# Pauses, loads and groups rearranged in the first quarter of a kernel for a 2-D transform and its experts

## The chip, the cores and the metric

The kernel runs on one core of a Trainium2 chip. What counts is the time of one execution on the device, in microseconds (us), smaller being better: the median of several runs. A kernel is compared with the kernel before on the same chip.

## The reference, cut to what matters

```python
def _attn_ref(x):                      # x: 8 batches, 2496 tokens, 256 columns
    X = np.fft.fft(x, axis=1)
    X = np.fft.fft(X, axis=2)
    return X.real.astype(np.float32)

def _moe_ref(x, w_gate, w1, w2):       # the 19968 tokens of the above, 8 experts, 1024 hidden
    logits = x @ w_gate
    expert_idx = np.argmax(logits, axis=1)
    ...                                # gate_w: the softmax value of the chosen expert
    for e in range(E):
        mask = expert_idx == e
        h = np.maximum(x[mask] @ w1[e], 0.0)
        out[mask] = gate_w[mask, None] * (h @ w2[e])
```

Every token is transformed, goes to the one expert with its largest logit, and its row comes back scaled.

## The kernel before, in words

**Transform.** A batch is folded by symmetry on VectorE (`fold_w`, `fold_fg`, `fold_z`, `fold_h`; lines 520 to 548), then multiplied along the sequence (S products, line 399, into two PSUM banks evicted by ScalarE's `ec` and VectorE's `pc`, `qc`, lines 452 to 464) and along the columns (D products, lines 758 to 767). A batch has two units, even and odd frequencies, so there are 16 units, numbered 0 to 15, each of 10 slots of 128 token rows. `load_x` (line 265) brings a batch in two DMAs of 1280 KB; there are two buffers for batches.

**Routing.** `route_a` and `route_b` find the expert of each token and its place in a list per expert; `place` (line 665) scatters each slot of 128 rows into `bucket` in HBM by an indirect DMA of GpSimd, ten of them a unit.

**Groups of tokens.** After units 2, 4, 7, 9, 11, 13, 15 and 16 a table says which rows of `bucket` make the next groups (`SEGS`: unit, width, number of groups). `first_row` and `group_rows` compute a table on VectorE, and `table_row` sends it to SyncE (line 1105), which reads registers from it (line 1124). The first four groups (0 to 3, `plain`) hold 128 rows, the next ten (4 to 13, "narrow" here) 256, later ones 512 ("tall"; from group 14 to 42 they are transposed on VectorE, line 1179, and not on TensorE). A group's rows are loaded by line 1136, its weights by line 1167 in eight parts of 256 KB, w1 and w2 of four parts each, into one buffer a part. So part p of the next group can be loaded only when this group has used its part p. The loads stand in SyncE's queue in program order, `x`, tables, rows and weights alike.

**Expert.** TensorE transposes the rows (line 1183), multiplies by w1 (line 1234 in plain groups; 1252 to 1254, three products of split operands, in others) and, two steps later, by w2 (1286; 1292 to 1295; 1302 and 1303). VectorE makes the low halves: `wal` of w1, `wb` of w2, `hl` of the hidden values, `xl` of the rows. `put` (line 1321) scatters the scaled rows to the output by indirect DMAs of GpSimd.

**Order.** In `start()`, units 0 to 3 and the first groups, the order on TensorE, VectorE and ScalarE is the program's own: `expert()` stands for one half step of the experts. After it `fft_until` steps are dealt between expert steps at a rate worked out from their counts, and a scheduler orders each engine's queue. Each engine takes its queue in order.

**Pauses of GpSimd.** `rest()` (lines 325 to 333) puts a fill of one element ahead of certain scatters and of each group's first `put`, and that fill waits until GpSimd's transfer before it has landed. `breath()` (lines 317 to 321) puts a fill of 128x1024 there, which waits for nothing, in units 1 to 3. Ahead of all, `start()` issues two indirect DMAs of no use to the result (`scrap`, line 809).

Of the kernel before, what the change touches and what calls it, by code (L numbers as in the profile page):

```python
# [22 lines left out]
P = 128  # L23
# [19 lines left out]
SEGS = [(2, 0.5, 4), (4, 1, 10), (7, 2, 4), (9, 2, 4), (11, 2, 5), (13, 2, 5), (15, 2, 5), (16, 2, 6)]  # L43
# [19 lines left out]
BLOCKED = 14, 43  # L63
PLAIN = 4
CUT = 2


def cuts():

    segs, used, g = [], 0, 0  # L70
    for n, w, count in SEGS:
        step, last = int(w * C), n == 2 * B
        rows = (n * H if g else int((~bad_slots()[:, : NE + CUT]).sum())) - used
# [151 lines left out]
def fft2_then_moe(ctx: ExitStack, tc: tile.TileContext, i: dict, out: bass.AP):  # L225
# [8 lines left out]
    scrap = dr.tile([S, P], I32, name="scrap")  # L234
# [73 lines left out]
    lull = cst.tile([1, 1], F32, name="lull")  # L308
    air = mo.tile([P, 2, 512], F32R, name="xl").bitcast(F32)
# [6 lines left out]
    def breath():  # L316

        last = ch["moved"]
        with tc.issue_after(last):
            pause = nc.gpsimd.memset(air, 0.0)  # L320
        return tc.issue_after(pause.ins)

    def rest():

        last = ch.get("moved")
        if not any(q is last for q in nc.cur_bb.bb.instructions):
            return nullcontext()
        with tc.issue_after(last):
# [4 lines left out]
        return tc.issue_after(pause.ins)  # L333
# [291 lines left out]
    def route_b(b, par, rb, st, fine=False):  # L625
# [14 lines left out]
        if (b, par) == (0, 1):  # L640
            ch["early"] = sc[:, :, CUT]
# [21 lines left out]
        def place(n, behind=None):  # L663
# [11 lines left out]
            tc.add_to_no_dep_group("sc1b" if u == 1 and n >= CUT else f"sc{u}", ins.ins)  # L675
# [19 lines left out]
    def groups_from(slots):  # L695

        return (["sc1b"] if slots <= NE + CUT else []) + [f"sc{q}" for q in range(-(-slots // NE), 2 * B)]

# [19 lines left out]
    def fft_steps():  # L718
# [88 lines left out]
        def start():  # L807
            for _ in range(2):
                nc.gpsimd.indirect_dma_start(
                    out=scrap[:, :],  # L810
                    out_offset=IndirectOffsetOnAxis(ap=ids[:, 0, 0:1].bitcast(U32), axis=0),
                    in_=ids.rearrange("p b n -> p (b n)")[:, 0:P],
                    in_offset=None,
                    bounds_check=S - 1,
                    oob_is_err=False,
                )
# [68 lines left out]
            pc = along_s_mm(2, 0)  # L885
            _, w, g0, count = cuts()[0]
# [5 lines left out]
            qc = along_s_mm(2, 1)  # L892
            pc()
# [6 lines left out]
            pc = along_s_mm(3, 0)  # L900
            st, rb = {}, cols.pop(2)
# [5 lines left out]
            qc = along_s_mm(3, 1)  # L907
# [18 lines left out]
            expert()  # L926
# [18 lines left out]
        for u, (b, par) in enumerate(units):  # L945
            if u < 4:
                continue
            if par == 0 and 2 <= b < B - 1:
                load_x(b + 1)
# [17 lines left out]
            yield from along_d(u)  # L967
# [47 lines left out]
    def group_rows(w, g0, count):  # L1015

        vec = nc.vector
        carry = ch["carry"]
# [110 lines left out]
    def load_rows(g):  # L1129
# [3 lines left out]
        xr = mo.tile([P, 4, RW], F32, name="xr", bufs=2)  # L1133
# [200 lines left out]
    def moe_steps(g0, g1):  # L1334
# [11 lines left out]
        if g0 == 0:  # L1346
            yield g0
# [4 lines left out]
        for n in range(len(units) + LAG):  # L1352
            if n < len(units):
                g, p, fs = units[n]
                more, half = g + 1 < g1, tall[g] == 1
                if p == 0 and fs[0] == 0 and more:
                    load_rows(g + 1)
# [44 lines left out]

    def begin():

        for g in first:
            rows_of[g] = ch["row", 2], NE + CUT
        next(moe)
# [7 lines left out]
    for n in sorted({s[0] for s in segs}):  # L1415
        todo = fft_until(n)
        if have:
            nf = FSTEPS * (n - rows_of[have[-1]][1] // NE)
# [33 lines left out]
        for g in have:  # L1452
            rows_of[g] = row, n * NE
# [29 lines left out]
```

## Time and profile before

| | |
|---|---|
| median of 3 runs | 1113.47 us (1109.48 to 1115.42) |
| the profiled execution | 1121.16 us |
| its span, first to last instruction | 1119.4 us |
| TensorE (PE) busy | 1066.6 us, 95% of the span |
| VectorE (DVE) busy | 810.1 us, 72% |
| ScalarE (ACT) busy | 592.2 us, 53% |
| GpSimd (POOL) busy | 359.4 us, 32% |
| mean granted clock of TensorE | 0.985 |

Busy time is a share of the whole span. The stages differ, so the sections below look at stretches of it. A row of the timeline gives start, duration, engine, source line, operation and tiles, and in square brackets how long the engine sat idle before it and what ended that. Duration of a merged row is from its first start to its last end.

### The profile page before, as it was taken

The numbers are of one execution on the slowest core, as the hardware profiler recorded it, in microseconds if no ns is written. First come the engines' busy times: TensorE is split into PE (matmuls) and PEld (weight loads), VectorE is DVE, ScalarE is ACT, GpSimd is POOL, SyncE is SP. The second block draws the span as 40 slices with busy tenths as digits, with TensorE's granted clock in tenths as the row PEclk, the third lists the DMA queues.
The fourth block names the chain that finished last, engine by engine and source line by source line (L and its number), as shares of the span: only waits on it lengthen the run. The fifth ranks groups of instructions, "written<-read, shape, count | busy, mean of one in ns | idle before, by whom it ended". The sixth has DMA issues, their size and how long they took to land.

```text
span 1119.4 us, 21641 instructions
## 1 busy us (share of the span) xinstructions
PE 1066.6 (95%) x6228; PEld 916.7 (82%) x6229; DVE 810.1 (72%) x1852; ACT 592.2 (53%) x1371; POOL 359.4 (32%) x407
## 2 busy tenths in 40 slices
PE   8686999999989999999999999999999999999997
PEld 4465898999878887888778887888888888899996
DVE  7745777977788698669766777678766666667775
ACT  2232465666554554455455555555555555466674
POOL 2754144541154235313531135311412111211111
PEclk9988999999999999999999999999999999999999
DMA  8559659745746466556564455445656555425511
GB/s 313 179 182 299 216 176 340 234 148 132 243 123 151 129 196 175 150 170 174 159 160 118 122 146 163 100 123 141 168 142 168 138 138 140 154 96 179 179 44 33
DMA packets 213431, 183.03 MB, mean 164 GB/s; under 512 B 150198, under 2 KB 153751, under 8 KB 211383
## 3 DMA queue, kind: packets, MB, share of 16 engines
q1 hardware_dynamic: 197171, 135.72, 45.0%
q0 software_dynamic: 15840, 45.67, 10.8%
q8 instruction: 51, 0.84, 0.3%
q14 instruction: 77, 0.63, 0.2%
q10 hardware_dynamic: 292, 0.17, 0.1%
HBM read 166.41 MB, written 45.07 MB: 189 GB/s over the span
## 4 chain that ended last, share of the span: by engine, by line
PE 82%; DVE 7%; DMA 4%; issue 3%; ACT 1%; SPq 1%; another core or an unknown queue 1%; POOL 0%; POOLq 0%; DVEq 0%; ACTq 0%
PE psY L1302 21%; PE psH L1253 12%; PE psH L1252 12%; PE psH L1254 11%; PE psY L1303 11%; PE psH L399 2%; PE psH L444 2%; PE psH L766 1%; PE psH L767 1%; DMA w1r<-w 1%; PE psY L1295 1%; PE psY L1294 1%; PE psY L1292 1%; DMA xr<-bucket 1%
## 5 line engine op out<-in xcount | busy, mean ns | idle before, releaser
L1302 PE MATMUL psY<-wb,hh 128*128 128x512 f32 x1088 | 397.6, 398 | 5.6 <-ACT hh L1257 2.3
L1321 POOL DMA_INDIRECT out<-ys,gt x160 | 165.2, 1033 | 446.1 <-DVE ys L1319 353.4
L1303 PE MATMUL psY<-wb,hl 128*128 128x256 f32 x1088 | 305.8, 281 | 0.2 <-DVE hl L1258 0.2
L1252 PE MATMUL psH<-xh,wah 128*128 128x512 f32 (+1 forms) x752 | 268.9, 358 | 3.1 <-ACT ec L452 1.7
L1253 PE MATMUL psH<-xl,wah 128*128 128x512 f32 (+1 forms) x752 | 264.6, 352 | 1.3 <-DVE xl L1193 1.1
L1254 PE MATMUL psH<-xh,wal 128*128 128x512 f32 (+1 forms) x752 | 262.5, 349 | 0.5 <-issue 0.3
L1302 PEld LDWEIGHTS psY<-wb,hh 128*128 128x128 f32 x1088 | 204.5, 188 | 52.4 <-issue 3.9
L1258 DVE SCALAR_TENSOR_TENSOR hl<-psH,hh 128x512 fp32r<-128x512 f32 (+1 forms) x320 | 215.1, 672 | 40.3 <-ACT hh L1257 34.5
L1257 ACT ACTIVATE hh<-psH 128x512 fp32r<-128x512 f32 (+1 forms) x320 | 187.7, 586 | 62.0 <-PE psH L1254 38.9
L665 POOL DMA_INDIRECT bucket<-rb,di x160 | 172.4, 1078 | 144.4 <-issue 65.3
L1303 PEld LDWEIGHTS psY<-wb,hl 128*128 128x128 f32 x1088 | 205.9, 189 | 8.4 <-DVE hl L1258 0.5
L1207 DVE TENSOR_TENSOR wal<-w1r,wah 128x512 fp32r<-128x512 f32 x188 | 129.5, 689 | 113.6 <-ACT wah L1206 87.8
L1206 ACT CAST wah<-w1r 128x512 fp32r<-128x512 f32 x188 | 117.0, 623 | 177.7 <-PE psH L1253 124.3
L1222 DVE TENSOR_TENSOR wb<-w2r,wb 128x512 fp32r<-128x512 f32 x204 | 140.0, 686 | 47.0 <-ACT wb L1221 38.1
L1221 ACT CAST wb<-w2r 128x512 fp32r<-128x512 f32 x204 | 127.8, 627 | 76.3 <-PE psY L1303 51.6
L1252 PEld LDWEIGHTS psH<-xh,wah 128*128 128x128 f32 x752 | 142.0, 189 | 25.0 <-issue 2.1
L1254 PEld LDWEIGHTS psH<-xh,wal 128*128 128x128 f32 x752 | 141.9, 189 | 21.1 <-issue 1.1
L1253 PEld LDWEIGHTS psH<-xl,wah 128*128 128x128 f32 x752 | 142.1, 189 | 12.9 <-DVE xl L1193 2.6
L1317 ACT ACTIVATE ys<-psY,gt 128x256 f32<-128x256 f32 x160 | 65.1, 479 | 9.3 <-PE psY L1295 4.3
L1192 ACT CAST xh<-psH 128x512 fp32r<-128x512 f32 x76 | 44.7, 588 | 40.7 <-DVE psH L1179 36.0
L1193 DVE TENSOR_TENSOR xl<-psH,xh 128x512 fp32r<-128x512 f32 x76 | 52.2, 687 | 11.6 <-ACT xh L1192 9.1
L1319 DVE SCALAR_TENSOR_TENSOR ys<-psY,gt,ys 128x256 f32<-128x256 f32 x136 | 56.8, 476 | 2.1 <-ACT ys L1317 2.1
(219 smaller groups left out, 1155.1 us busy)
## 6 DMA issues: line engine op xcount, KB each, us to landing
w1r<-w SPq DMA_DIRECT2D x220, 256.0 KB
w2r<-w SPq DMA_DIRECT2D x220, 256.0 KB
x<-xin SPq DMA_DIRECT2D x12, 1280.0 KB
xr<-bucket SPq DMA_DIRECT2D x232, 64.0 KB
xr<-bucket SPq DMA_DIRECT2D x18, 266.0 KB
x<-xin SPq DMA_DIRECT2D x3, 1024.0 KB
bucket<-rb,di POOLq DMA_INDIRECT x160
out<-ys,gt POOLq DMA_INDIRECT x160
```

What stands on the lines that cost most here:

```text
L665: ins = nc.gpsimd.indirect_dma_start(out=bucket[:, :], out_offset=IndirectOffsetOnAxis(ap=di[:, n : n + 1].bitcast(U32), axis=0), in_=rb[: ...
L1207: nc.vector.tensor_sub(lo, src, hi.bitcast(F32))
L1221: nc.scalar.copy(wb[:, :, 0], src)
L1222: nc.vector.tensor_sub(wb[:, :, 1], src, wb[:, :, 0].bitcast(F32))
L1252: nc.tensor.matmul(o, lhsT=wh[:, c], rhs=xh[:, k, :], start=(k == 0), stop=False)
L1253: nc.tensor.matmul(o, lhsT=wh[:, c], rhs=xl[:, k, :], start=False, stop=False)
L1254: ch["mm"] = nc.tensor.matmul(o, lhsT=wl[:, c], rhs=xh[:, k, :], start=False, stop=(k == 1))
L1257: nc.scalar.activation(hh[:, z], hp[:, z], AF.Relu)
L1258: nc.vector.scalar_tensor_tensor(out=hl[:, z], in0=hp[:, z], scalar=0.0, in1=hh[:, z].bitcast(F32), op0=ALU.max, op1=ALU.subtract)
L1302: nc.tensor.matmul(y, lhsT=hh[:, c], rhs=wide_w, start=(first and q == 0), stop=end, skip_group_check=True)
L1303: nc.tensor.matmul(y[:, 0:D], lhsT=hl[:, c], rhs=wb[:, f, 0], start=False, stop=end, skip_group_check=True)
L1321: ins = nc.gpsimd.indirect_dma_start(out=out, out_offset=IndirectOffsetOnAxis(ap=gt[:, a, 1:2].bitcast(U32), axis=0), in_=ys, in_offset=No ...
```

## The change

1. `rest()` becomes three fills of 128x320 (into `xg`, no longer needed then) that wait for no landing, and takes the place of `breath()` too. It also leaves out unit 0.
2. The two `scrap` DMAs go.
3. The second table counts only the first 36 tiles (six slots of unit 3, `CUTS`), and its groups' loads wait for those scatters alone. It makes 8 narrow groups instead of 10, and the third table makes 5 tall ones instead of 4: one group less in all.
4. The rows of the four plain groups are loaded together, at the first group, into one tile.
5. Batch 3, the fourth, comes in four loads of 640 KB (`load_part`) during the D products of unit 4, and not in two at that unit's beginning.
6. In `start()`: six more products of no use to the result (`hold`) behind each S product of unit 2; both S products of unit 3 together; fewer expert steps between the D products and the routing of unit 3.

```diff
-SEGS = [(2, 0.5, 4), (4, 1, 10), (7, 2, 4), (9, 2, 4), (11, 2, 5), (13, 2, 5), (15, 2, 5), (16, 2, 6)]
+SEGS = [(2, 0.5, 4), (4, 1, 8), (7, 2, 5), (9, 2, 4), (11, 2, 5), (13, 2, 5), (15, 2, 5), (16, 2, 6)]
-BLOCKED = 14, 43
+BLOCKED = 12, 42
-CUT = 2
+CUTS = {1: 2, 3: 6}
...
+    def load_part(b, q):
+        if b not in xs_of:
+            xs_of[b] = ff.tile([P, 4, 5, 256], F32, name="x")
+        with after("sp"):
+            ch["sp"] = nc.sync.dma_start(out=xs_of[b][:, q], in_=i["xin"][b][:, q]).ins
...
-    air = mo.tile([P, 2, 512], F32R, name="xl").bitcast(F32)
+    air = xg.rearrange("p q c -> p (q c)")
...
-        with tc.issue_after(last):
-            pause = nc.gpsimd.memset(lull, 0.0)
-        tc.add_manual_dep(
-            pause.ins, last.name, mybir.DependencyInfo(mybir.DependencyClass.Sync, mybir.DependencyReason.DATA), reason="a pause between transfers"
-        )
-        return tc.issue_after(pause.ins)
+        for _ in range(3):
+            with tc.issue_after(last):
+                last = nc.gpsimd.memset(air, 0.0).ins
+        return tc.issue_after(last)
...
+    def hold(n):
+
+        wp = ps.tile([P, 512], F32, name="psH", bufs=4)
+        for _ in range(n):
+            nc.tensor.matmul(wp, lhsT=ones, rhs=busy, start=True, stop=True)
...
-            stop = rest() if not fine and n in (0, 4, 8) else breath() if fine and u and n in (0, 5) else follow(not fine or u > 0)
+            stop = rest() if n in ((0, 5) if fine else (0, 4, 8)) and u else follow(not fine or u > 0)
...
             pc = along_s_mm(2, 0)
+            hold(6)
...
             qc = along_s_mm(2, 1)
+            hold(6)
...
             pc = along_s_mm(3, 0)
+            qc = along_s_mm(3, 1)
             st, rb = {}, cols.pop(2)
...
             expert()
-            qc = along_s_mm(3, 1)
             run(rb2)
...
-            for _ in along_d(3, (0, 2, 4)):
-                expert()
+            for kt, _ in enumerate(along_d(3, (0, 2, 4))):
+                if kt in (1, 3):
+                    expert()
                 next(fb)
...
-                if n % 2:
+                if n in (1, 3):
                     expert()
...
-            expert()
+            expert(2)
             run(rb3)
...
-            if par == 0 and 2 <= b < B - 1:
+            if par == 0 and 2 < b < B - 1:
                 load_x(b + 1)
...
-            yield from along_d(u)
+            for kt, _ in enumerate(along_d(u)):
+                if u == 4 and kt < 4:
+                    load_part(3, kt)
+                yield
...
-        carry = ch["carry"]
+        carry = ch["early"] if g0 == PLAIN else ch["carry"]
...
         if g0 == 0:
+            for g in range(1, PLAIN):
+                load_rows(g)
             yield g0
```

The change moves instructions. Three places matter below.

SyncE's queue, around the loads of batch 3 (`x`) and of group 3's rows (the `xr` of 128x266). Before, behind the second table's row:

```order
L1105 DMA row<-tab 1x66x4
L265 DMA x<-xin 128x2560 x2
L1124 TENSOR_LOAD row_595
L1124 ISA x2
L1136 ISA
L1136 DMA xr<-bucket 128x266
L1124 TENSOR_LOAD row_595
```

After, the batch stands further on, behind the load of group 4's rows, among group 4's weights (`w1r_126` to `w1r_128`, `w2r_130`) and group 3's last two parts of w2:

```order
L273 DMA x<-xin 128x1280
L1172 ISA
L1172 DMA w1r_127<-w 128x512
L273 DMA x<-xin 128x1280
L1172 ISA
L1172 DMA w2r_133<-w 128x512
L273 DMA x<-xin 128x1280 x2
L1172 ISA
L1172 DMA w1r_128<-w 128x512
L1172 ISA
L1172 DMA w2r_130<-w 128x512
L715 DMA bucket<-c_pad 16x4256 x8
```

The batch moved from ahead of group 3's rows to behind group 4's, and those of groups 1 to 3 moved up to behind group 0's weights.

TensorE's queue, from the routing of unit 2 (L629 before, L631 after) on; L399 and L401 are S products of unit 3, the first with `xr` the transposes of group 0, L758 to L767 and L761 to L770 the D products of unit 3. Before:

```order
L1183 MATMUL psH<-pack,xr 128x128 x2
L1234 MATMUL psH<-xh,w1r_129 128x128 x4
L399 MATMUL psY_783<-cs_72,x 128x313 x2
L399 MATMUL psY_784<-cs_72,x 128x313 x2
L399 MATMUL psY_783<-cs_72,x 128x313
L399 MATMUL psY_784<-cs_72,x 128x313
L1234 MATMUL psH<-xh,w1r_130 128x128 x4
L758 MATMUL psH<-pack,pc 128x137
```

After:

```order
L401 MATMUL psY_752<-cs_71,x 128x313 x2
L401 MATMUL psY_753<-cs_71,x 128x313 x2
L401 MATMUL psY_752<-cs_71,x 128x313
L401 MATMUL psY_753<-cs_71,x 128x313
L631 LDWEIGHTS trib
L631 MATMUL psH<-ohb,trib 128x80
L632 LDWEIGHTS ones
L632 MATMUL psH<-ohb,ones 128x80
L1188 MATMUL psH<-pack,xr 128x128 x2
L1239 MATMUL psH<-xh,w1r_126 128x128 x4
L1239 MATMUL psH<-xh,w1r_127 128x128 x4
L761 MATMUL psH<-pack,pc 128x137
```

The second S product of unit 3 moved from behind group 0's first expert step to ahead of the routing of unit 2.

VectorE's queue, at the fold of batch 3 (the `x` of 128x2x512, L520 before, L522 after). Before, it stood behind the second table and ahead of all work of narrow groups:

```order
L1101 TENSOR_TENSOR tab<-tacc 128x1
L459 TENSOR_TENSOR pc<-ec,psH 128x313
L462 TENSOR_TENSOR pc<-ec,psH 128x312
L1100 MEMSET tab 128x1
L520 TENSOR_TENSOR x<-x 128x2x512
L1199 COPY gt<-xr 128x1
L520 TENSOR_TENSOR x<-x 128x2x512
```

After, it stands among group 4's halves (`wal` of part 2, `hl` of part 0, `wb` of part 0):

```order
L650 TENSOR_TENSOR lg<-psH,sc 128x80
L522 TENSOR_TENSOR x<-x 128x2x512
L653 TENSOR_TENSOR lg<-lg,ohf 128x80
L1212 TENSOR_TENSOR wal<-w1r_128,wah 128x512
L1263 SCALAR_TENSOR_TENSOR hl<-psH,hh 128x512
L656 TENSOR_REDUCE dst<-lg 128x10
L1227 TENSOR_TENSOR wb<-w2r_130,wb 128x2x256
```

The fold moved behind the first of group 4's work on VectorE.

## Rows read from the trace of the kernel before

**Rows 1.** Busy time by stretch: us, then PE, PEld, DVE, ACT, POOL, PEclk, DMA share, GB/s.

```profile
53.80:59.10 5.30, 5.28 (x31) 5.28 (x32) 3.42 (x7) 1.20 (x6) 4.39 (x4) 0.68 0.82 206
59.10:75.10 16.00, 11.80 (x49) 7.82 (x47) 8.03 (x29) 5.34 (x20) 7.90 (x9) 0.79 0.55 171
75.10:99.40 24.30, 22.82 (x158) 20.42 (x159) 13.80 (x61) 9.35 (x35) 14.23 (x15) 1.00 0.77 220
99.40:109.95 10.55, 0.78 (x5) 0.39 (x3) 0.71 (x2) 0.38 (x1) 4.98 (x6) 0.63 1.00 376
109.95:115.67 5.72, 5.72 (x22) 4.57 (x22) 5.69 (x11) 0.85 (x3) 1.52 (x2) 0.50 0.72 230
...
128.50:252.00 123.50, 118.44 (x952) 113.50 (x951) 97.32 (x228) 78.95 (x187) 53.63 (x63) 1.00 0.69 223
252.00:1119.40 867.40, 848.40 (x4732) 729.94 (x4731) 628.25 (x1359) 473.89 (x1036) 244.77 (x276) 1.00 0.52 144
```

**Rows 2.** Waits of TensorE: us in total, times, longest us.

```profile
PE psH L1183 <- DMA xr<-bucket: 9.8, 1, 9.8
```

**Rows 3.** Timeline of SyncE's queue at group 3's rows.

```profile
95.97 0.94 SPq L265 DMA_DIRECT2D x<-xin  x2
98.01 0.35 SPq L1136 DMA_DIRECT2D xr<-bucket  x1
```

**Rows 4.** Timeline of VectorE, first and last row of the fold of batch 3.

```profile
109.30 1.23 DVE L520 TENSOR_TENSOR x<-x 128x1024 f32<-128x1024 f32 x1 [9.70 <-DMA x<-xin]
...
120.62 0.69 DVE L548 TENSOR_TENSOR x<-x 128x512 f32<-128x512 f32 x1
```

**Rows 5.** Timeline of TensorE, from unit 1's routing to unit 3's S products.

```profile
40.72 2.27 PE L382 MATMUL psY<-pack,ones 128*128 128x512 bf16 x5 [2.60 <-DVE mx L588]
...
49.04 0.80 PE L399 MATMUL psY<-cs,zs 128*128 128x156 f32 x4 [2.21 <-DVE x L535]
...
53.82 0.50 PE L759 MATMUL psH<-nsd,qc 128*128 128x136 f32 x2 [2.29 <-issue]
...
64.75 0.22 PE L629 MATMUL psH<-ohb,trib 128*128 128x80 bf16 x1 [2.68 <-ACT ohb L609]
...
67.85 4.83 PE L399 MATMUL psY<-cs,x 128*128 128x313 f32 x12
```

**Rows 6.** Timeline of VectorE, unit 3: evictions of its S products, and its scatter addresses.

```profile
69.44 0.48 DVE L459 TENSOR_TENSOR pc<-ec,psY 128x313 f32<-128x313 f32 x1 [1.93 <-ACT ec L452]
...
74.53 0.48 DVE L459 TENSOR_TENSOR qc<-ec,psY 128x313 f32<-128x313 f32 x1 [3.55 <-ACT hh L1238]
...
90.71 0.16 DVE L658 TENSOR_TENSOR di<-dst,pack 128x10 int32<-128x10 f32 x1
```

**Rows 7.** Busy time of one narrow group and of an eighth of a tall one.

```profile
860.84:863.60 2.76, 2.76 (x17) 2.35 (x15) 2.66 (x6) 2.17 (x6) 1.25 (x2) 1.00 0.81 269
140.54:152.77 12.23, 12.23 (x104) 12.12 (x103) 9.28 (x18) 8.44 (x17) 3.89 (x4) 1.00 0.62 190
```

**Rows 8.** Timeline of GpSimd: unit 0's first scatter; the pause behind unit 3's ten.

```profile
29.53 1.26 POOL L665 DMA_INDIRECT bucket<-rb,di  x1 [11.59 <-DVE pc L459]
...
111.53 0.09 POOL L329 MEMSET lull<- 1x1 f32 x1 [5.77 <-DMA bucket<-rb,di]
```

**Rows 9.** Timeline of SyncE's queue at group 0's rows.

```profile
59.84 0.01 SPq L1136 DMA_DIRECT2D xr<-bucket  x1
```

**Rows 10.** Waits of GpSimd's pauses for landings: us in total, times, longest us.

```profile
POOL lull L329 <- DMA bucket<-rb,di: 78.3, 26, 5.8
...
POOL lull L329 <- DMA out<-ys,gt: 46.3, 18, 4.2
```

**Rows 11.** Timeline, a long fill of GpSimd and small operations of VectorE beside it and apart.

```profile
45.23 0.98 POOL L320 MEMSET xl<- 128x1024 f32 x1
...
45.46 0.78 DVE L989 TENSOR_SCALAR ni<-ni 128x8 int32<-128x8 int32 x1
...
435.39 0.17 DVE L1023 TENSOR_SCALAR ni<-ni 128x8 int32<-128x8 int32 x1
```

More of the change, by code (lines that the diff above doesn't have):

```diff
@@ L72, in cuts @@
         step, last = int(w * C), n == 2 * B
-        rows = (n * H if g else int((~bad_slots()[:, : NE + CUT]).sum())) - used
+        q = (n - 1) % 2 * NE
+        rows = (n - 1) * H + int((~bad_slots()[:, q : q + CUTS.get(n - 1, NE)]).sum()) - used
         assert last or count <= max(0, -(-(rows - E * (step - 1)) // step))
@@ L233, in fft2_then_moe @@
     bucket = dr.tile([ROWS, RW], F32, name="bucket")
-    scrap = dr.tile([S, P], I32, name="scrap")
     cs0 = cst.tile([P, 2, 3, M], F32, name="cs0")
@@ L307, in fft2_then_moe @@
     sent = []
-    lull = cst.tile([1, 1], F32, name="lull")
-    air = mo.tile([P, 2, 512], F32R, name="xl").bitcast(F32)
+    air = xg.rearrange("p q c -> p (q c)")
     def follow(on):
@@ L314, in follow @@
         return tc.issue_after(last) if on and any(q is last for q in nc.cur_bb.bb.instructions) else nullcontext()
-    def breath():
-        last = ch["moved"]
-        with tc.issue_after(last):
-            pause = nc.gpsimd.memset(air, 0.0)
-        return tc.issue_after(pause.ins)
     def rest():
@@ L327, in rest @@
             return nullcontext()
-        with tc.issue_after(last):
-            pause = nc.gpsimd.memset(lull, 0.0)
-        tc.add_manual_dep(
-            pause.ins, last.name, mybir.DependencyInfo(mybir.DependencyClass.Sync, mybir.DependencyReason.DATA), reason="a pause between transfers"
-        )
-        return tc.issue_after(pause.ins)
+        for _ in range(3):
+            with tc.issue_after(last):
+                last = nc.gpsimd.memset(air, 0.0).ins
+        return tc.issue_after(last)
     trib = cst.tile([P, P], BF16, name="trib")
@@ L639, in route_b @@
         )
-        if (b, par) == (0, 1):
-            ch["early"] = sc[:, :, CUT]
+        if 2 * b + par in CUTS:
+            ch["early"] = sc[:, :, CUTS[2 * b + par]]
         ch["carry"] = sc[:, :, NE]
@@ L674, in place @@
                 tc.declare_no_dep(ins.ins, group=g, reason="the rows of tokens are distinct")
-            tc.add_to_no_dep_group("sc1b" if u == 1 and n >= CUT else f"sc{u}", ins.ins)
+            tc.add_to_no_dep_group(f"sc{u}b" if n >= CUTS.get(u, NE) else f"sc{u}", ins.ins)
             if behind is not None:
@@ L695, in groups_from @@
     def groups_from(slots):
-        return (["sc1b"] if slots <= NE + CUT else []) + [f"sc{q}" for q in range(-(-slots // NE), 2 * B)]
+        late = [f"sc{u}b" for u, cut in CUTS.items() if slots <= u * NE + cut]
+        return late + [f"sc{q}" for q in range(-(-slots // NE), 2 * B)]
     def drop(behind):
@@ L807, in start @@
         def start():
[L808 to L816, printed above, removed]
             spin(WARM)
@@ L1132, in load_rows @@
         base = reg(row, 4 * g, ROWS - P * n)
-        xr = mo.tile([P, 4, RW], F32, name="xr", bufs=2)
+        if plain(g):
+            if g == 0:
+                ch["early rows"] = mo.tile([P, 4, RW], F32, name="xr", bufs=2)
+            xr = ch["early rows"][:, g : g + 1]
+        else:
+            xr = mo.tile([P, 4, RW], F32, name="xr", bufs=2)
         rows = bucket[ds(base, P * n), :]
@@ L1356, in moe_steps @@
                 if p == 0 and fs[0] == 0 and more:
-                    load_rows(g + 1)
+                    if not plain(g + 1):
+                        load_rows(g + 1)
                     w_regs(g + 1)
@@ L1401, in fft2_then_moe, with tiles @@
     moe = moe_steps(0, SURE)
+    def tiles(n):
+        return (n - 1) * NE + CUTS.get(n - 1, NE)
     def begin():
         for g in first:
-            rows_of[g] = ch["row", 2], NE + CUT
+            rows_of[g] = ch["row", 2], tiles(2)
         next(moe)
@@ L1417, in fft2_then_moe @@
         if have:
-            nf = FSTEPS * (n - rows_of[have[-1]][1] // NE)
+            nf = FSTEPS * (n + -rows_of[have[-1]][1] // NE)
             stop = have[-1]
@@ L1452, in fft2_then_moe @@
         for g in have:
-            rows_of[g] = row, n * NE
+            rows_of[g] = row, tiles(n)
     for _ in range(8 * (SURE - 2 - ch["at"]) + sum(8 for g in range(ch["at"], SURE - 2) if tall[g] == 4)):
```

## The prediction

> **What bounds the kernel now.** Read the stretches first [rows 1]. From 252 us to the end TensorE is busy 848.4 of 867.4 us, 98%, at full clock: little is to be had there. In the narrow groups, 128.5 to 252, it is busy 118.44 of 123.5. Ahead of 128.5 lie the holes. The worst is 99.40 to 109.95: 0.78 us of work in 10.55, while the DMA share is 1.00 at 376 GB/s. Then come 5.72 us in which TensorE is busy throughout at a clock of 0.50, the lower of its two levels: the same work at full clock is half as long.
>
> Then ask what ended that hole. TensorE waited once, 9.8 us, for the rows of group 3 [rows 2]. SyncE issued them at 98.01, right behind the two loads of batch 3 at 95.97 [rows 3]: 133 KB that ended their wait at 109.95, some 12 us after their issue, behind 2 x 1280 KB. VectorE stood too: the fold of batch 3 waited 9.70 us and began at 109.30 [rows 4]. That 2560 KB at 376 GB/s take 7.0 us, and other transfers were under way, fits both. So the path through this stretch is a load that stands behind another on one queue.
>
> **The change part by part.** The sum is made against the profiled execution, 1121.16 us, which lies 7.7 us (0.7%) above the median of 1113.47; the gains are carried over to the median unchanged.
>
> *Rows loaded together, batch 3 later.* Group 3's rows are now issued at group 0's place, which was 59.84 [rows 9], some 40 us ahead of their use, and no load of `x` stands before them. The wait of 9.8 us goes. What is late next is group 4, taken up below. **-9.8**. The clock of 0.50 followed the hole [rows 1]; without the hole I take it as full: 5.72 x 0.5 = **-2.9**.
>
> *Units 2 and 3.* From 59.10 to 75.10 TensorE did 11.80 us of work in 16.00, clock 0.79 [rows 1], and 2.68 us of it was a wait for unit 2's routing on ScalarE [rows 5]. Both S products of unit 3, of which 12 in a row took 4.83 us [rows 5], now stand ahead of that wait or in it; before, the second stood behind group 0's step, so that its eviction `qc` came at 74.53, 5.1 us after `pc` at 69.44 [rows 6]. The 2.68 us are filled. Further, 53.80 to 59.10 held 5.28 us of work at 0.68: at full clock 3.6, so 1.7 less, if the `hold` products keep the engine at work before it. Of the work at 0.79 as much as 11.80 x 0.21 = 2.5 could go; I take a quarter, 0.6, since weights must still land there (share 0.55). Together **-5.0**; bounds: -2.7 (the wait alone) and 4.2 idle + 1.7 + 2.5 = -8.4.
>
> *Groups.* Eight narrow groups for ten is 2 x 12.23 = 24.5 us less; a tall one more is 8 x 2.76 = 22.1 [rows 7]. **-2.4**; down to nothing if the extra tall group waits for its weights. Fewer weights move, too: eight parts of 256 KB.
>
> These four make -20.1. Two things give some back.
>
> *VectorE in the narrow stretch.* It was busy 97.32 of 123.5 us there [rows 1], and the fold of batch 3, from 109.30 to 120.62 [rows 4] with some other work between, hence 10 us of its own, lay ahead of it. Now the fold stands behind the first halves of group 4, inside it. Two narrow groups less take 2 x 8 away (9.28 us in one's window [rows 7], a little of it the transform's): 97.3 - 16 + 10 = 91 us in some 99, 92% for 79%. TensorE idled 5.06 us there [rows 1] and I give it **+4** more; bounds 0 and +10 (the whole fold).
>
> *The batch on SyncE's queue.* The four loads of `x`, 7.0 us of transfer, and eight pads now stand among the weights of group 4 and the last of group 3. What stands behind them is late by up to 7.0 us, and the buffers ahead cover a part: **+2.5**; bounds 0 and +9.8, a wait as long as the one removed. The trace shows what such a place costs, in the 12 us of group 3's rows. The Trainium skill ("DMA: Bandwidth & Descriptors", section "Queues, rings and completion order") has it that a DMA engine serves its queues in turn, and the descriptors of one ring start in order. By that rule cutting a load in four helps nothing that stands behind all four, and my give-back would be nearer its upper end; the trace agrees as far as it goes, with those 12 us.
>
> *Priced at nothing.* The `hold`: 12 products of 128x512. Five products of that shape took 2.27 us, 0.45 each, and two waits of TensorE, 2.21 and 2.29 us, stand about where they go [rows 5]; 12 x 0.45 = 5.4 less 4.5 leaves 0 to 1 us uncovered. The `scrap`: GpSimd idled 11.59 us for VectorE before its first scatter [rows 8]; taken away, two issues free no one. The later second table (36 tiles and not 40) waits for fewer scatters: before, the last pause behind unit 3's ten stood 5.77 us for a landing till 111.53 [rows 8], and narrow groups could not start ahead of it; that is part of the hole that is already counted.
>
> *The pauses.* Three fills of 128x320. No such row is in the trace: one element took 0.09 us [rows 8], 128x1024 took 0.98 [rows 11], so 0.09 to 0.98; I take 0.31, the second's by length, since one element shows little but the fixed part. A pause, three fills, is 0.9 us (0.3 to 2.9). Before, 44 pauses waited 78.3 + 46.3 = 124.6 us for landings [rows 10], 2.8 each. GpSimd is busy 32% of the span and was no releaser in the holes of TensorE above, so this is 0 on the path; gains and losses have their rivals. One rule speaks against more fills: while a fill of 0.98 us ran from 45.23, a small VectorE operation begun at 45.46 lasted 0.78 us and ended as the fill did, while one of its kind took 0.17 alone [rows 11]. The Trainium skill ("SBUF — State Buffer", section "Who interferes with whom") says that GpSimd and VectorE's copies and scalar operations lock each other out of a shared port for a whole instruction. By row and rule alike the price is one such stretch, at most 0.3 us a fill of the new length, and only where VectorE is what TensorE waits for: under 1 us.
>
> **The sum.** -9.8 - 2.9 - 5.0 - 2.4 + 4 + 2.5 = -13.6: 1113.5 - 13.6 = **1100** (the profiled execution would be 1107.5).
>
> **The rivals.** *Nothing is given back:* -20.1, **1093**. For it: the two narrow groups gone. Against it: a fold that now stands ahead of group 4's own halves on an engine that goes in order. *VectorE becomes the bound of the narrow stretch:* +10 for +4, **1106**. For it: 92%; against: 79% before left 5 us of holes. *The wait only moves:* the batch lands as late as before, and the fold, now between group 4's halves, holds TensorE for up to the 9.8 us, with half clock after it, so that the first -12.7 are lost, and -5.0 - 2.4 + 4 = -3.4 stays: **1110**, no change that can be told. For it: the DMA share of 1.00 says that the bytes, not only their order, were late. Against it: from 128.5 the share is 0.69, so there is room for 7.0 us. *The change does not do what it says:* group 3's rows would be late for another reason, the backlog at the scatters of unit 3; then only the last terms stay, **1111**. Its address rows were done at 90.71 [rows 6], its last landing 111.53, so scatters were late too, but group 3's rows come from unit 2 at the latest, which speaks against it.
>
> *Slower, by the pauses:* without waits for landings the scatters of 44 places follow each other after 0.9 us and not 2.8, pile up on the DMA engines, and hold the weights up. If each place costs TensorE 0.6 us, 26 us are lost, and -13.6 + 26 gives **1126**. It outweighs the gain from (13.6 + 5.6) / 44 = 0.44 us a place. For it: nothing else keeps GpSimd back. Against it: a DMA share of 0.52 from 252 us on [rows 1].
>
> **How the numbers follow.** Forecast 0.50 (its own range 1095 to 1105), nothing given back 0.11, VectorE the bound 0.16, the wait moves 0.13, not what it says 0.03, slower 0.07. Half a per cent, 5.6 us, is about what a measurement of this kernel can tell from no change: faster is below 1107.9, no change up to 1119. That makes 0.77, 0.16 and 0.07. The range, 1091 to 1111, reaches from the best case (with 2 us for its unknown prices) to the wait that moves and the change without effect; outside stay the slow case, 0.07, and the far ends of the others, some 0.1.
>
> **What would show it.** In the profile after: no TensorE wait for rows of group 3; a granted clock near 1.00 from 54 us through the plain groups; six and six S products of unit 3 in one row, the wait before unit 2's routing short. Group 4 would start near 112 and not 128.5. The give-backs would show as TensorE waits on `x` folds, `wal`, `wb` or `hl` in the first narrow groups, with VectorE over 90% there. A fill of 128x320 should read about 0.3 us, and GpSimd have no wait for a landing at a pause. From 252 us on TensorE should be at 98% as before. It is wrong if the first narrow group starts later than 120, if weights wait more in the tall groups, or if the gain is found behind 252 us.

## The result, and the profile after

The changed kernel took 1125.2 us (median of 4, 1118.5 to 1131.0) where the kernel before, on the same chip, took 1111.47: a ratio of 1.0138, 95% interval 1.0097 to 1.0179 (the two medians alone would give 1.0124). It is slower; 1100 and a range of 1091 to 1111 were forecast. The profiled execution took 1118.50 us, its span is 1116.6 us. The experiments ran on several chips, on which the kernel before has medians from 1096 to 1119 us; so they are compared by their ratio to the kernel before on the same chip, and never by their microseconds. Experiments e1 to e4 share one chip, e5 to e8 a second, e9 to e12 a third, e13 to e16 a fourth, e17 and e18 a fifth; the changed kernel as it stands ran only for the result and in e1. Ratios are of executions in the fast state alone; one execution of e6 took 3689.8 us and is left out with the slow ones.

First, the two parts of the span that differ. The view is busy time by stretch (us, then PE, PEld, DVE, ACT, POOL, granted clock, DMA share, GB/s), of the changed kernel:

```profile
0.00:140.00 140.00, 120.67 (x743) 92.79 (x744) 96.81 (x298) 51.97 (x184) 70.99 (x96) 0.99 0.79 267
140.00:200.00 60.00, 49.63 (x363) 46.40 (x362) 44.56 (x113) 31.55 (x88) 35.99 (x42) 0.91 0.76 263
```

and the same two stretches in a second execution of the kernel before (experiment e5):

```profile
0.00:140.00 140.00, 111.19 (x646) 84.65 (x647) 93.44 (x290) 46.39 (x169) 61.20 (x71) 0.93 0.72 241
140.00:200.00 60.00, 56.66 (x444) 54.78 (x443) 46.45 (x105) 36.83 (x99) 24.57 (x30) 0.94 0.77 260
```

Call the time that is not spent at work at full clock (the stretch, less busy time by granted clock) lost. Ahead of 140 us the loss falls from 140 - 111.19 x 0.93 = 36.6 us to 140 - 120.67 x 0.99 = 20.5: 16 us gained, about what was forecast there (17.7). Between two executions on one chip, e3 (the kernel before with new pauses) and e1 (the changed kernel), it falls by 12 us only; and busy time here includes the twelve `hold` products, 2.9 us in the changed kernel, which are of no use to the result. From 140 to 200 the loss rises from 6.7 to 14.8. The wait for group 3's rows [rows 2] is gone, and group 4 starts at 109.37.

Now ask what ended the new hole. The rows below show, in the changed kernel, SyncE at the next batch (batch 4, two loads of 1280 KB) and at a narrow group's rows; then GpSimd's two loads of tables for the odd frequencies (1570 KB each, first used at 228 us); then VectorE's fold of batch 4; and last TensorE:

```profile
144.93 0.90 SPq L265 DMA_DIRECT2D x<-xin  x2
146.67 0.35 SPq L1141 DMA_DIRECT2D xr<-bucket  x1
```

```profile
145.51 0.63 POOL L436 DMA_DIRECT2D cs1l<-c_cs1l  x1
...
155.38 0.61 POOL L436 DMA_DIRECT2D cs<-c_cs  x1
```

```profile
160.82 1.23 DVE L522 TENSOR_TENSOR x<-x 128x1024 f32<-128x1024 f32 x1 [4.79 <-DMA x<-xin]
```

```profile
162.96 1.08 PE L1188 MATMUL psH<-pack,xr 128*128 128x128 f32 x4 [4.39 <-DVE qc L466]
```

This is the picture of [rows 2 to 4] once more, one batch later: rows 1.7 us behind a batch on one queue, a fold that waits for the batch, TensorE idle. The wait is put down to VectorE's `qc`, whose end came last; the same wait in a second execution (e1) is put down to the rows themselves:

```profile
147.96 0.35 SPq L1141 DMA_DIRECT2D xr<-bucket  x1
```

```profile
164.59 1.09 PE L1188 MATMUL psH<-pack,xr 128*128 128x128 f32 x4 [4.76 <-DMA xr<-bucket]
```

That wait ended 16.6 us after the rows were issued, and the fold of batch 4 began 15.9 us (in e1 16.6) after the batch was issued. Around the wait the granted clock falls; windows of the changed kernel, ahead of the wait and from it on:

```profile
150.00:158.00 8.00, 7.41 (x59) 6.70 (x58) 5.39 (x17) 4.13 (x10) 4.49 (x7) 1.00 1.03 407
158.00:172.00 14.00, 8.15 (x39) 7.66 (x38) 6.92 (x12) 3.98 (x13) 6.12 (x7) 0.63 0.97 365
```

14 us hold 8.15 x 0.63 = 5.1 us of work at full clock, so 8.9 are lost, with a DMA share of 0.97. In e1 the clock of this stretch is 0.88, and 7.4 are lost.

Was this to be seen ahead of the run? The rows of SyncE's queue were. In the kernel before, batch 4 stands a weight part away from the rows, and in the profile its load went out at 165.41 and the rows at 171.16:

```
L265 DMA x<-xin 128x2560 x2
L1167 ISA
L1167 DMA w2r_135<-w 128x512
L1124 TENSOR_LOAD row
L1124 ISA x2
L1136 ISA
L1136 DMA xr<-bucket 128x532
```

In the changed kernel, right ahead of them:

```
L265 DMA x<-xin 128x2560 x2
L1124 TENSOR_LOAD row
L1124 ISA x2
L1141 ISA
L1141 DMA xr<-bucket 128x532
```

### The profile page after: what moved, and what is told of

The parts are those of the page before. It is cut to its first block, busy times and chain, and to the rows that moved or that the text cites. A ratio compares the mean times of both kernels' runs of the same rounds, so it can differ in the third digit from the quotient of the medians.

```text
span 1116.6 us, 21544 instructions
## 1 busy us (share of the span) xinstructions
PE 1069.4 (96%) x6153; PEld 911.8 (82%) x6153; DVE 808.6 (72%) x1848; ACT 587.9 (53%) x1361; POOL 413.1 (37%) x516
## 3 DMA queue, kind: packets, MB, share of 16 engines
q0 software_dynamic: 15776, 45.43, 10.7%
## 4 chain that ended last, share of the span: by engine, by line
PE 84%; DVE 5%; DMA 5%; issue 2%; ACT 2%; SPq 1%; another core or an unknown queue 0%; POOL 0%; POOLq 0%; DVEq 0%; ACTq 0%
PE psY L1307 22%; PE psH L1257 12%; PE psH L1258 12%; PE psH L1259 12%; PE psY L1308 11%; DMA x<-xin 2%; PE psH L401 2%; PE psH L446 2%; PE psH L769 1%; PE psH L770 1%; DMA w2r<-w 1%; DMA w1r<-w 1%; PE psH L1239 1%; PE psY L401 1%; PE psY L1297 1%
## 5 line engine op out<-in xcount | busy, mean ns | idle before, releaser
L1307 PE MATMUL psY<-wb,hh 128*128 128x512 f32 x1120 | 411.8, 401 | 3.3 <-DVE ys L1324 2.1
L1326 POOL DMA_INDIRECT out<-ys,gt x160 | 168.0, 1050 | 506.4 <-DVE ys L1324 415.8
L1308 PE MATMUL psY<-wb,hl 128*128 128x256 f32 x1120 | 314.3, 281 | 0.9 <-issue 0.6
L1307 PEld LDWEIGHTS psY<-wb,hh 128*128 128x128 f32 x1120 | 210.5, 188 | 53.3 <-DVE ys L1324 2.9
L1308 PEld LDWEIGHTS psY<-wb,hl 128*128 128x128 f32 x1120 | 211.4, 189 | 10.2 <-DVE hl L1263 1.1
L1212 DVE TENSOR_TENSOR wal<-w1r,wah 128x512 fp32r<-128x512 f32 x184 | 126.6, 689 | 118.3 <-ACT wah L1211 97.8
L1227 DVE TENSOR_TENSOR wb<-w2r,wb 128x512 fp32r<-128x512 f32 x200 | 136.8, 684 | 41.0 <-ACT wb L1226 31.3
L1257 PEld LDWEIGHTS psH<-xh,wah 128*128 128x128 f32 x736 | 139.3, 189 | 28.0 <-issue 4.2
L1258 PEld LDWEIGHTS psH<-xl,wah 128*128 128x128 f32 x736 | 139.5, 190 | 13.8 <-issue 2.1
L328 POOL MEMSET xg<- 128x320 f32 x168 | 62.9, 374 | 6.3
L1198 DVE TENSOR_TENSOR xl<-psH,xh 128x512 fp32r<-128x512 f32 x76 | 52.2, 687 | 11.6 <-ACT xh L1197 9.1
```

Of the source, the lines that this page charges most:

```text
L1212: nc.vector.tensor_sub(lo, src, hi.bitcast(F32))
L1227: nc.vector.tensor_sub(wb[:, :, 1], src, wb[:, :, 0].bitcast(F32))
L1257: nc.tensor.matmul(o, lhsT=wh[:, c], rhs=xh[:, k, :], start=(k == 0), stop=False)
L1258: nc.tensor.matmul(o, lhsT=wh[:, c], rhs=xl[:, k, :], start=False, stop=False)
L1307: nc.tensor.matmul(y, lhsT=hh[:, c], rhs=wide_w, start=(first and q == 0), stop=end, skip_group_check=True)
L1308: nc.tensor.matmul(y[:, 0:D], lhsT=hl[:, c], rhs=wb[:, f, 0], start=False, stop=end, skip_group_check=True)
```

## The experiments

Each ratio is to the kernel before on the same chip, with its 95% interval.

**e1, the changed kernel once more.**

> The changed kernel once more, for a second profile and more times. If the loss is in the granted clock of single executions, a slower execution than 1118.5 us shows more time at the half clock than the 9 us from 163 to 172, and the place where it falls. If the change costs 1.2% steadily, the ratio to the kernel before is 1.010 to 1.017 again, and the stall of 4.4 us before group rows at 158 us, with half clock behind it, is in this profile too.

Ratio 1.0102 (1.0069 to 1.0134); its profiled execution took 1122.9 us. The wait stands at the same place (above). So the loss is steady, and it is no matter of the mean granted clock: that is 0.9875 over these runs, against 0.9857 for the kernel before.

**e2, the old pauses in the changed kernel, and e3, the new pauses in the old one.**

```diff
# e2
-        for _ in range(3):
-            with tc.issue_after(last):
-                last = nc.gpsimd.memset(air, 0.0).ins
+        with tc.issue_after(last):
+            pause = nc.gpsimd.memset(lull, 0.0)
+        tc.add_manual_dep(pause.ins, last.name, ...)
...
-            stop = rest() if n in ((0, 5) if fine else (0, 4, 8)) and u else ...
+            stop = rest() if not fine and n in (0, 4, 8) else breath() if fine and u and n in (0, 5) else ...
```

> The changed kernel with the pauses of before (one element, waiting for the landing, and the long fill in units 1 to 3). Theory 'pauses': the fills that wait for no landing let transfers pile up on the weights; then this is faster than the changed kernel by 10 us or more, 1100 to 1114. Theory 'batch 4': the loss is the load of the fifth batch, which now comes at 145 us and not 165; then this is within 5 us of the changed kernel, 1120 to 1130, and the stall near 158 stays.

> The kernel before with the new pauses alone (three fills of 128x320, no wait for a landing); the two first transfers without use stay. Theory 'pauses': slower than the kernel before by 10 us or more, 1121 to 1130. Theory 'batch 4': within 5 us of the kernel before, 1107 to 1117.

e3: 1.0002 (0.9976 to 1.0029). e2: 1.0177 (1.0144 to 1.0210), on the chip of e1, and its interval lies clear above that of e1. The theory "pauses" falls on both sides: the fills cost the kernel before nothing, and in the changed kernel they are worth some 0.7%. Where: stretch 60 to 100, of e2 and then of e1.

```profile
60.00:100.00 40.00, 29.59 (x179) 26.11 (x178) 20.76 (x87) 12.54 (x46) 24.34 (x25) 0.87 0.58 185
```

```profile
60.00:100.00 40.00, 32.15 (x208) 27.41 (x207) 17.42 (x75) 13.07 (x48) 30.80 (x43) 0.96 0.70 222
```

That is 40 - 29.59 x 0.87 = 14.3 us lost, against 9.1, and unit 4's first scatter comes 8.1 us later. Why is not shown: the pauses of units 1 to 3 are fills in both versions, and from 55 to 105 us GpSimd waits for one landing only, 1.5 us. TensorE's longest wait there, 4.5 us at unit 3's routing, has no named releaser. The wait for rows behind batch 4 stays in e2 as it was forecast:

```profile
174.28 1.08 PE L1198 MATMUL psH<-pack,xr 128*128 128x128 f32 x4 [4.40 <-DMA xr<-bucket]
```

**e4, batch 4 in four loads too, one unit part later; e7 and e8, the same earlier.**

```diff
# e4
-            if par == 0 and 2 < b < B - 1:
+            if par == 0 and 3 < b < B - 1:
                 load_x(b + 1)
...
-                if u == 4 and kt < 4:
-                    load_part(3, kt)
+                if u in (4, 6) and kt < 4:
+                    load_part(b + 1, kt)
# e7: u in (4, 5), load_part(u - 1, kt)
# e8: parts 0 and 1 in the D products of unit 5, parts 2 and 3 behind the S products of unit 6
```

> The changed kernel with the fifth batch (batch 4) also loaded in four parts, during the D products of unit 6 and not ahead of that unit. Theory 'batch 4': the wait of 4.4 us near 158 us and the 9 us of half clock behind it go, and some of the VectorE wait of 4.8; 6 to 12 us less than the changed kernel, 1113 to 1119. Theory 'pauses': within 4 us of it.

> The changed kernel with batch 4 in four loads during the D products of unit 5, some 10 us earlier than now. Theory 'batch 4 ahead of a group's rows': the group's rows come in time, no wait near 158 us, DMA under 1.0 of share in 150 to 180; 1100 to 1110, better than the kernel with its four loads in unit 6. Rival 'the bytes are too many there in any order': within 4 us of that kernel, 1107 to 1114.

> The changed kernel with batch 4 in four loads, two during the D products of unit 5 and two behind the S products of unit 6. Theory 'batch 4 ahead of a group's rows': as good as or better than four in the D products of unit 5, 1100 to 1110. Rival 'the bytes are too many': 1107 to 1114.

e4: 1.0015 (0.9988 to 1.0041). Its parts go out from 157.93 to 169.23, and the wait ahead of the group's rows is gone:

```profile
140.00:200.00 60.00, 54.93 (x425) 53.00 (x424) 48.90 (x126) 37.22 (x98) 39.24 (x46) 0.94 0.81 279
```

60 - 54.93 x 0.94 = 8.4 lost, against 14.8 and 15.8 (e1). On the chip of e1 this takes the ratio from 1.0102 to 1.0015, so there the load of batch 4 is where the change loses. But e7, 1.0088 (1.0044 to 1.0132), and e8, 1.0092 (1.0060 to 1.0125), with the parts from 139 and from 141 us, are no better than the 1.0102 of e1: an earlier load gains nothing that can be told, though the group's rows go out some 3 us behind the last part in e7. Both theories expected more of them. In e8 the wait moved again: VectorE stood 12.41 us ahead of the fold of batch 4, whose last part had gone out at 157.21, and TensorE waited 10.7 us for the `wal` behind that fold in VectorE's queue. The profile names nothing that ended VectorE's wait, so that it was the batch is argued from the order alone.

```profile
170.54 1.23 DVE L522 TENSOR_TENSOR x<-x 128x1024 f32<-128x1024 f32 x1 [12.41 <-issue]
PE psH L769 <- DVE wal L1216: 10.7, 1, 10.7
```

**e5, the kernel before once more, and e6, only the rows of the plain groups together.**

```diff
# e6, in the kernel before
...
         if g0 == 0:
+            for g in range(1, PLAIN):
+                load_rows(g)
             yield g0
...
-                    load_rows(g + 1)
+                    if not plain(g + 1):
+                        load_rows(g + 1)
```

> The kernel before once more, for a second profile. If the holes ahead of 128 us are the same in each execution, TensorE again waits some 10 us for group 3's rows with 5 to 6 us of half clock behind it, and unit 4's first scatter comes at 143 us. If the profile shown was an unlucky execution (it lies 10 us above the median), the wait is under 7 us, and that scatter comes by 138.

> The kernel before with only the rows of the four plain groups loaded together; batch 3 stays where it was. Theory 'rows behind the batch': the wait of TensorE for group 3's rows goes, 9.8 us and the half clock behind it, 1095 to 1103. Theory 'the wait only moves' (the fold and group 4's weights behind the same batch, or batch 4 later): 1105 to 1113.

e5 has the wait of [rows 2] again, 9.0 us, and unit 4's first scatter at 139.65 (143.40 in the profile shown): most of the hole is there in each execution. e6: 0.9959 (0.9926 to 0.9993), which is 4.5 us (0.8 to 8.2) for the rows alone, where rows and batch 3 together were forecast at 9.8 + 2.9. Waits of TensorE, of e6:

```profile
PE psH L1239 <- DMA w1r<-w: 6.5, 1, 6.5
```

With the rows out of the way it is a part of w1, behind the same two loads of 1280 KB, that comes late. Both theories are half right: the wait gets shorter, by 2.5 us against e5, and changes its name. In the changed kernel, where batch 3 moved too, neither wait is there.

**e9 to e11, the tables later.**

```diff
# e9 and e11; e10 is e9 on top of e4
-                if u == THREE - 1:
-                    odd_table(1 - q)
                 along_s(u, q)
...
+                if u == THREE - 1 and kt in (2, 4):
+                    odd_table(int(kt == 2))
                 yield
```

> The changed kernel with the two 1570 KB tables of the odd frequencies, which GpSimd now issues at 145 and 155 us beside the load of batch 4, issued in the D products of unit 6 instead; the batch stays where it is. They are first used at 228 us. Theory 'tables and batch at once': 3140 KB less in 145 to 165 let the rows behind the batch land in time, no wait near 158 us, 1105 to 1113. Rival 'order on SyncE's queue alone': the rows still come some 14 us after their issue, 1117 to 1124.

> The same, with batch 4 in four loads in the D products of unit 6 as well. Theory 'tables and batch at once': both gains or the better of the two, 1098 to 1108. Rival 'order on SyncE's queue alone': as the kernel with those four loads alone, 1107 to 1114, or worse if the tables now meet the batch again.

> The kernel before with the tables late alone. There the batch is issued 5.8 us ahead of a group's rows and TensorE lost 3 to 5 us in 170 to 200. Theory 'tables and batch at once': up to those 3 to 5 us less, 1104 to 1110. Rival: no change.

e9: 1.0012 (0.9976 to 1.0047). The batch goes out at 148.11 and the rows 1.74 us behind it, as in the changed kernel; only the tables have moved, to 172.09 and 175.08. The fold now begins 12.3 us after the batch was issued, and TensorE takes the rows 11.6 us after their issue, without a wait:

```profile
148.11 0.90 SPq L265 DMA_DIRECT2D x<-xin  x2
149.85 0.35 SPq L1141 DMA_DIRECT2D xr<-bucket  x1
160.41 1.23 DVE L522 TENSOR_TENSOR x<-x 128x1024 f32<-128x1024 f32 x1 [1.38 <-DMA x<-xin]
161.41 0.60 PE L1188 MATMUL psH<-pack,xr 128*128 128x128 f32 x4
172.09 0.62 POOL L436 DMA_DIRECT2D cs1l<-c_cs1l  x1
```

The longest wait of TensorE left in 130 to 210 is one of 3.1 us, ahead of a product by w1 at 170.58, with no named releaser. So the order on SyncE's queue alone does not make the rows late; the tables on GpSimd's queue in the same 15 us do. (That the ratio fell by this is likely and not shown, as the changed kernel did not run on this chip.) e10 moves batch and tables into the same D products, and they meet again: 1.0078 (1.0045 to 1.0112), with

```profile
140.00:200.00 60.00, 48.94 (x358) 46.00 (x357) 41.87 (x106) 31.18 (x86) 32.83 (x39) 0.89 0.82 275
```

16.4 us lost. This cannot be put down to the meeting: one of its two longest waits, 4.4 us, ended at 172.22, half a us after the first table went out, and e13 below, without the meeting, is no better within the intervals. e11: 0.9995 (0.9954 to 1.0036); in the kernel before the tables' place is worth nothing that can be told.

**e13, both apart, and e18, e4 on another chip.**

```diff
# e13, on top of e4: the tables behind the scatters of unit 6
-                if u == THREE - 1:
-                    odd_table(1 - q)
                 along_s(u, q)
...
                 late = None
+                if u == THREE - 1:
+                    odd_table(1)
+                    odd_table(0)
                 ch["done"] = u + 1
```

> The changed kernel with batch 4 in four loads in the D products of unit 6, and the tables issued behind the scatters of unit 6, some 30 us after the batch and ahead of their use at 228. Theory 'the meeting is the whole of the loss': no stall in 150 to 200, the gain ahead of 128 us stays, 0.985 to 0.995 of the kernel before. Rival 'something else gives the gain back': 0.998 or more.

> The changed kernel with batch 4 in four loads in the D products of unit 6, once more. Theory 'batch 4 beside the tables and ahead of a group's rows is the loss': ratio 0.998 to 1.005 again. Rival 'the first result was this chip's luck': 1.006 to 1.014, as the changed kernel.

e13: 1.0061 (1.0019 to 1.0103). With the tables at 207.72, TensorE still waits 5.8 us in 160 to 180, at a DMA share of 0.9:

```profile
PE psH L1258 <- DVE hl L1264: 5.8, 1, 5.8
172.20 0.62 ACT L1212 CAST wah<-w1r 128x512 fp32r<-128x512 f32 x1 [5.14 <-remote]
```

This wait is the end of a chain: ScalarE idled 5.14 us, from 167.06 to 172.20, ahead of a cast of w1. Its releaser is not named ("remote"). A late part of w1 behind the batch does not explain it: the next load of w1 went out at 172.13, and the one before at 158.74, ahead of the batch's parts, which went out from 159.76 on. So "the meeting is the whole of the loss" falls, and what holds the engines here stays open. e18: 1.0053 (1.0037 to 1.0068) where e4 had 1.0015. Its middle is just past the bound of its theory, and in its profile TensorE waits again for a group's rows, which went out behind three of the four parts, at 159.46:

```profile
175.04 1.08 PE L1188 MATMUL psH<-pack,xr 128*128 128x128 f32 x4 [4.15 <-DMA xr<-bucket]
```

So batch 4 in parts does not always free the rows; by the two chips it takes back from half to nearly all of the 1.0 to 1.4%.

**e14 and e17, groups and tables of the change, taken away and alone.**

```diff
# e14, in the changed kernel (e17: the reverse, in the kernel before)
-SEGS = [(2, 0.5, 4), (4, 1, 8), (7, 2, 5), ...
+SEGS = [(2, 0.5, 4), (4, 1, 10), (7, 2, 4), ...
-BLOCKED = 12, 42
+BLOCKED = 14, 43
-CUTS = {1: 2, 3: 6}
+CUTS = {1: 2}
...
-        carry = ch["early"] if g0 == PLAIN else ch["carry"]
+        carry = ch["carry"]
```

> The changed kernel with the groups and tables of before (ten narrow groups, second table behind all of unit 3). Theory 'the earlier table and the other deal brought the meeting ahead of a group's rows': unit 4 and 6 come later against the groups, the batch is issued 4 us or more ahead of a group's rows as before, and the loss is mostly gone, ratio 0.995 to 1.003. Rival 'it is the rest of the change': ratio 1.008 or more.

> The kernel before with only the groups and tables of the change (SEGS, BLOCKED, CUTS, and the second table that counts 36 tiles); rows, batches, pauses and the order in the first four units stay. Theory 'the other deal costs it': ratio 1.008 to 1.015, and a wait of TensorE or half clock in 140 to 200 that the kernel before has not. Rival 'only beside the earlier start of the rest': 0.997 to 1.004.

e14: 0.9996 (0.9965 to 1.0028). Batch 4 goes out at 156.82, the rows 4 us behind it, the tables at 159.41 and 166.59. TensorE takes these rows at 174.24 without a wait, and the loss against the kernel before is gone (and so is any gain).

```profile
156.82 0.84 SPq L265 DMA_DIRECT2D x<-xin  x2
160.86 0.35 SPq L1141 DMA_DIRECT2D xr<-bucket  x1
174.24 0.60 PE L1188 MATMUL psH<-pack,xr 128*128 128x128 f32 x4
```

So batch and tables meet here as well, as they do in the kernel before (165.41, then 168.06 and 175.86), and nothing is late. What differs is the time until the rows are asked for: 17.4 us after the batch was issued in e14, 18.2 in the kernel before, 13.6 in the changed kernel, whose rows came after 18.0. That this slack decides is read from these profiles and was not tested by itself. e17: 1.0027 (1.0016 to 1.0037): alone, the new groups cost 3 us. There too the rows stand 1.8 us behind the batch (150.91 and 149.15), and TensorE waits:

```profile
PE psH L768 <- DVE hl L1260: 3.3, 1, 3.3
PE psH L1185 <- DMA xr<-bucket: 2.9, 1, 2.9
```

So this part of the change is what moves the load of batch 4 to right ahead of a group's rows; the full 1% it costs only beside the rest, which brings unit 4's first scatter to 125 us (e1: 128.58) where e17 has it at 133.97.

**e12 and e16, without `hold`; e15, rows together and tables later in the kernel before.**

```diff
# e12 on top of e10, e16 on top of e13
-            hold(6)
# e15: e6, and the tables as in e13
```

> As the kernel with tables late and batch 4 in four loads, without the 12 products that hold TensorE. If they keep the clock at full in 40 to 65 us, their going costs the half clock there, 4 to 6 us more. If they only fill waits, no change or up to 2.6 us less (12 x 0.21).

> As the changed kernel with both loads apart, without the 12 products that hold TensorE. If they earn the clock they keep, 3 us or more worse than with them; if they only take their own time, up to 2.6 us better.

> The kernel before with only the rows of the plain groups together and the tables behind the scatters of unit 6. The rows alone gave 0.996. Theory 'the meeting costs here too' (3 to 5 us in 170 to 200): 0.991 to 0.995. Rival: 0.996 again.

e12: 1.0044 (1.0001 to 1.0087) beside 1.0078 with the products; e16: 1.0090 (1.0048 to 1.0131) beside 1.0061. One each way, inside the intervals: no effect of the `hold` can be told. e15: 0.9993 (0.9951 to 1.0036): 0.9959 lies inside, so this neither repeats nor refutes the gain of e6. No version was found that is clearly faster than both kernels; e6, with its few lines, is the only one whose interval lies under 1, barely.

## Why the prediction was wrong

Progress is best read from two starts on GpSimd: unit 4's first scatter (the transform) and the 40th scatter to the output (four or five tall groups done; units 0 to 8 are scattered in all by then, so the work behind is alike). The three kernels with e in front ran on one chip; us.

| kernel | unit 4's first scatter | 40th to the output | span |
|---|---|---|---|
| e3 (before, new pauses; ratio 1.0002) | 136.68 | 385.07 | 1112.2 |
| e1 (changed) | 128.58 | 391.10 | 1120.9 |
| e4 (changed, batch 4 later, in parts) | 126.67 | 377.39 | 1105.6 |
| changed, first profile | 125.03 | 387.69 | 1116.6 |

e1 is 8.1 us ahead of e3 at unit 4 and 6.0 behind at the 40th scatter: 14 us lost between. e4 keeps 7.7 of its 10.0. From there to the end all four take 727 to 730 us. (e4's profiled execution was the fastest of its ten, e1's the slowest of its four and e3's above its median, so the last column shows more than the medians do.) Of the 14 us some 11 lie from 140 to 200. A second place was in no theory and was not tested: from 318 to 340, at the first tall groups, e1 loses 4.8 us by busy time and clock, the first profile 4.9, but e4 1.8 and e3 0.9. The rows are of e1, then e4:

```profile
318.00:340.00 22.00, 18.68 (x80) 14.14 (x79) 16.11 (x44) 9.40 (x19) 17.01 (x23) 0.92 0.59 151
318.00:340.00 22.00, 20.22 (x103) 16.79 (x102) 19.26 (x50) 11.31 (x22) 13.35 (x19) 1.00 0.53 157
```

*Rows together, batch 3 later (-9.8, -2.9).* In the changed kernel this came as forecast: the wait went, and group 4 started at 109.37 for a forecast of 112. It took both parts: with the rows alone (e6) a part of w1 behind the batch is late, 6.5 us, and 4.5 us are gained (0.8 to 8.2).

*Units 2 and 3 (-5.0).* In the right direction: the loss ahead of 140 us fell by 12 to 16 us, this term and the last together. They were not measured apart.

*Groups (-2.4).* Wrong in sign: alone, +3.0 us (e17, 0.0027 x 1096). The two prices compared windows of 12.23 and 2.76 us [rows 7]; the products of two narrow groups and one tall have the same columns in sum (96 + 96 of 256, and 32 + 48 of 512 and 32 of 256: 49152 each), so little could be saved on TensorE, and where the deal then puts a batch was not priced at all.

*VectorE in the narrow stretch (+4).* Not as forecast: from 128.5 to 200 it is busy 54.54 of 71.5 us, 76% and not 92%. It stood 4.79 us for the batch ahead of the fold, and the longest wait of TensorE is that for rows and `qc`; its other waits there are of 1.5 us and less.

```profile
128.50:200.00 71.50, 60.11 (x444) 56.47 (x445) 54.54 (x132) 39.31 (x105) 41.61 (x49) 0.93 0.78 269
```

*The batch on SyncE's queue (+2.5, bounds 0 and 9.8).* **This is the step that failed.** It priced batch 3 at its new place, where nothing was late (VectorE's fold of it began at 113.38 without a wait). A wait of the same kind as the one removed, half as long, came at batch 4, which the edit does not touch, and whose place follows from the other groups and from a transform that runs earlier. For the other batches the sum has no term: their loads were put at nothing without a reason. In its place the runs show a wait of 4.4 to 4.8 us with a lower clock around it, 8 to 11 us more lost from 140 to 200, and a ratio that falls from 1.0102 to 1.0015 when batch 4 alone is moved. The rival "the wait only moves" had the mechanism, with 0.13 and the wrong batch, and stopped at 1110, since it let nothing behind it get worse. The rule cited there (the Trainium skill, "DMA: Bandwidth & Descriptors", section "Queues, rings and completion order") fits what was found: rows behind a batch on SyncE's queue came 16.6 us after their issue in e1, and GpSimd's tables, on another queue, decide in e9 whether they are in time.

*The pauses (0).* Right for the kernel before, 1.0002, and the rival "slower, by the pauses" is refuted by e3: that its 1126 lies next to the measured 1125.2 is luck. A fill of 128x320 took 0.374 us on average for the 0.31 forecast, 168 of them 62.9 us, and no pause waits for a landing. In the changed kernel they help (e2), which was not forecast.

```profile
L328 POOL MEMSET xg<- 128x320 f32 x168 | 62.9, 374 | 6.3
```

*What stays open.* That the place of batch 4's load makes most of the loss is shown by e4 against e1 on one chip; e18, on another, leaves half of it, and e14 fits. That the tables beside it make the rows late is shown by e9, in one version. It is neither enough by itself (e14, and the kernel before) nor the whole (e13, e18). What holds the engines in e13, why parts of batch 4 that go out earlier (e7, e8) do no good, and what the place from 318 to 340 costs, was not settled. No run took batch 3 in parts, the order of the first four units or the `scrap` alone. Open too are 2 to 3 us at the very end: from the 140th scatter to the output on, the changed kernel takes 123.0 us, e1 123.1 and e14 123.0, where e5 takes 120.2 and e3 120.8.

## What to carry to other kernels

When a change takes a load out from ahead of something, look at every other load of its kind and what now stands right behind it on its queue, in the changed order and not in the edit: an order that is dealt from counts moves them all. Price the removal of a wait by what is late next at the same place (here a part of w1, when the rows alone were moved), and test it alone. And ask of a large load how long after it the rows behind it are wanted: here 13 to 14 us were too few with other large loads on another queue beside it and enough without them (e9), and 17.4 were enough with them (e14).

## What the runs showed of the hardware

Loads on another queue delayed a queue's own: with 3140 KB of GpSimd's tables in the same 15 us as 2560 KB on SyncE's queue, TensorE got rows issued 1.7 to 2.0 us behind the batch only 16.2 to 16.7 us after their issue (the changed kernel, e1, e2, e17); with the tables 18 to 27 us later it had them within 11.6 us (e9). And TensorE's busy time did not measure its progress: from 400 to 1000 us the changed kernel shows 597.35 us busy and the kernel before (e5) 593.60, while the 100 scatters to the output from the 40th to the 140th took 606 us in both (387.69 to 993.65, and 385.23 to 991.11).
